# A linear-attention and mixture-of-experts kernel: where g tiles and raw weights lie, the order of the first 16 slots, and the diagonals of the first units on ScalarE

## Chip, core and metric

One core of a Trainium2 chip runs the whole program in one launch. The metric is the device time of that core in microseconds, median over runs.

## What is computed

Three stages over 3072 tokens (4 sequences of 768, 8 heads of 48):

```
for t in range(S):                                   # stage 1, per batch and head
    y[t]  = r[t] @ (state + outer(u * k[t], v[t]))
    state = w[t][:, None] * state + outer(k[t], v[t])
x = y as [3072, 384]
h = x @ w_in                                         # stage 2, 384 -> 2048 -> 384
x1 = (h * tanh(softplus(h))) @ w_out
logits = x1 @ w_gate                                 # stage 3, 8 experts, 384 tokens each
assign tokens to experts greedily, largest logit first, until an expert is full
out[mask_e] = relu(x1[mask_e] @ w1[e]) @ w2[e]
```

## The kernel before, in words

**Units.** Stage 1 is cut into 24 units of 128 columns (two sequences side by side, 64 steps each). `att0` (L341) makes running products of w by a scan on VectorE and the product `rk`; `att_inv` their inverses on ScalarE; `att1` and `att1b` scale r and k in place; `att_K` transposes k into `kn`; `att_A` multiplies k with r into PSUM tile `A`; `bon1` and `bon2` make the bonus terms `bT` and `bt`; a tile `Dt` is built as a diagonal (identity times `bt`, L387) into which `copy_predicated` puts the masked part of `A`; `att_S` moves the state on; `att4` (y, L463) multiplies `Dt` with v, writes the unit's outputs as two f16 halves into `xg` and starts the loads of later units.

**Weights.** `w_in` and `w_out` arrive as f64 in 16 slices. `conv` (L491) turns a slice into f32 with three VectorE instructions; `split` (L500) writes the f16 high half on ScalarE (L504) and the low half on VectorE (L505). Slices 0 to 7 give `wi`, 8 to 15 give `wo`. A raw slice lies in a buffer that `raw_of` (L243) chooses: 2 to 5 in the still empty `wo`, 6 to 9 in tiles of pool `p_g`, 0, 1 and 10 to 15 in a ring of two in pool `p_cv`. `og_T` (L517) and `og_M` (L529) multiply w_out with w_gate, so that eight more columns of `wo` give logits.

**Slots.** Tokens are taken in 12 groups of 256 (two units each). A slot is one eighth of a group's first layer: `mm1` (L547), 18 matmuls with 256 columns, then a tanh and a scaled copy. Four slots make a half, on which `act_ln`, `act_sin`, `act_he` and `act_g` (L568 to L601) leave the tile `g` as f16 high and low. The second layer is a stream of 384 parts (`mm2_part`, L605), three matmuls each, 32 to a group; `mm2` (L719) draws from it after each slot so many as the tables `rate` and `beat` say. For groups below `ND0` a part has 392 columns, of which eight are the logits `V`; for the others `logits` (L634) and `logits_sum` (L652) compute these apart.

**Order.** Nothing is scheduled by a tool. Every step has a key in slots, in the table `CFG`; all steps are sorted by it (L752) and written out in that order, which each engine follows. `CFG["dve"]` says for each kind of small copy which indices go to VectorE; the rest go to ScalarE. `warm` (L334) issues dummy matmuls of 512 columns on TensorE, 108 in all. TensorE's first 37 have nothing else in front.

**Gate and experts.** After the last slot, `gate` finds thresholds by 22 rounds of counting, `make_idx` writes the token index of each expert slot, both on VectorE with small matmuls; at each of their pauses TensorE takes some of the remaining parts (`amount`). The index then drives gathers of x1 rows, 30 dummy matmuls (`hold`) and the eight experts.

Of the kernel before, what the change touches and what calls it, by code (L numbers as in the profile page):

```python
# [18 lines left out]
P = 128  # L19
# [4 lines left out]
CFG = {'conv': [-27.465, -26.239, -0.642, 0.355, 1.387, 1.774, 3.754, 5.116, 5.48, 6.31, 6.977, 7.807, 8.631, 10.369,  # L24
          10.592, 11.496],
 'split': [-27.205, -24.825, 0.807, 1.381, 2.26, 3.003, 4.163, 5.354, 5.902, 7.352, 7.913, 8.296, 8.882, 11.157,
           11.265, 12.47],
 'ogT': [6.752, 8.458, 9.9, 10.25, 11.129, 11.882, 12.619, 12.917],
 'ogM': [8.177, 9.662, 10.2, 10.602, 11.386, 11.899, 12.819, 14.749],
 'u': ({'att0': -3.415,  # L30
        'bon1': -2.42,
        'bon2': -0.705,
        'inv': 1.465,
        'r1': 1.47,
        'k1': 1.491,
# [24 lines left out]
        1: {'att0': -20.044,  # L60
            'inv': -19.909,
            'r1': -19.677,
            'bon1': -19.214,
            'k1': -18.359,
            'K': -17.218,
            'A1': -17.179,
            'bon2': -18.264,
            'S': -16.813,
            'y': -15.438},
        2: {'att0': -19.14,  # L70
            'inv': -18.95,
# [36 lines left out]
            'A1': 6.016,
            'S': 7.667},
        6: {'att0': -3.862, 'bon1': -2.537, 'bon2': -0.898},  # L110
        7: {'att0': -1.258, 'bon1': -1.188, 'bon2': -0.407}},
 'rate': [(9, 0), (16, 20), (78, 200), (81, 201), (89, 209), (88, 219), (93, 232), (99, 258)],
 'beat': (16, 80, (9, 3, 0, 0, 2, 0, 0, 7)),
 'close_cv': 15.0,
 'close_att': 86.65,
 'mm1': 0.724,
 'mm2': 1.324,
 'half': ({'at': -2.795, 'sin': (-0.016, -0.015), 'he': (0.269, 0.464), 'g': (1.712, 3.088)},
          {'at': -0.109, 'sin': (0.379, 0.536), 'he': (0.613, 1.164), 'g': (3.652, 5.128)}),
 'halves': {},  # L120
 'begin': {('warm', 0): -33.78,
           ('wg',): 5.6,
           ('ld', 4): -25.706,
           ('ld', 5): -25.98,
           ('ld', 6): -24.091,
           ('ld', 7): -21.7,
           ('ld', 8): -23.6,
           ('ld', 9): -23.974,
           ('warm', 1): -24.946,
           ('warm', 2): -24.041,  # L130
           ('warm', 3): -1.989,
           ('warm', 4): 4.794,
           ('warm', 5): 9.244,
           ('warm', 6): 9.808},
 'warm': [37, 12, 14, 20, 15, 2, 8],
 'amount': {'I0': 3, 'I1': 0, 'g': 1, 't': 6, 'c': 3, 'o': 11},
# [7 lines left out]
         'ghi': {33, 4, 37, 5, 9, 13, 45, 17, 21, 25, 29, 31},  # L144
# [7 lines left out]
 'alone': {9},  # L152
 'lg': 7.167,
 'hold': 30}
# [3 lines left out]
def tile_rwkv_mish_greedy_moe(  # L158
# [47 lines left out]
    p_o = ctx.enter_context(tc.tile_pool(name="p_o", bufs=2, side="right"))  # L206
    p_cv = tc.tile_pool(name="p_cv", bufs=1, side="right")
# [35 lines left out]
    def raw_of(i):  # L243
        if 2 <= i < 6:
            t = spare[:, (i - 2) * KD * CW:(i - 1) * KD * CW]
        elif 6 <= i < 10:
            t = p_g.tile([P, 2, NF // 2, G], F16, name="g").rearrange("p a f g -> p (a f g)")
            t = t.bitcast(mybir.dt.int64)[:, 0:KD * CW]
        else:
            t = pc.tile([P, KD * CW], mybir.dt.int64, name="raw", bufs=2)  # L250
        return t
# [89 lines left out]
    def att0(n):  # L341
# [8 lines left out]
        (nc.vector if on_v("rk", n) else nc.gpsimd).tensor_tensor(rk, Tps["r", n], Tps["k", n], op=ALU.mult)  # L350
# [28 lines left out]
    def bon2(n):  # L379
        pb = pq.tile([P, C], F32, name="Y", bufs=2)  # L380
        made.add("whole")
        nc.tensor.transpose(pb, bTs.pop(n), ident)
        bt = pa.tile([P, 2, NP], F32, name="bt")
        move("bT", n, bt, pb.rearrange("t (p j) -> t j p", j=32)[:, 0:2, :])
        bt = bt.rearrange("t j p -> t (j p)")
        Dt[n] = pa.tile([P, H, L], F32, name="Dt")
        (nc.vector if on_v("Dt", n) else nc.gpsimd).tensor_tensor(Dt[n], diag[:, None, :].to_broadcast([P, H, L]),  # L387
                                bt[:, :, None].to_broadcast([P, H, L]), op=ALU.mult)

    def att1b(n):  # L390
# [3 lines left out]
        (nc.vector if on_v("nt", n) else nc.gpsimd).tensor_tensor(nt, inv, E_of(n)[:, :, 1:], op=ALU.mult)  # L394
# [67 lines left out]
    def att4(n):  # L462
# [838 lines left out]
```

## Time and profile before

| | us |
|---|---|
| median of 3 runs | 836.95 (836.71 to 838.04) |
| profiled execution, own time | 836.1 |
| its span | 834.4 |
| TensorE matmul busy | 762.4 (91%) |
| VectorE busy | 548.4 (66%) |
| ScalarE busy | 452.8 (54%) |
| mean granted TensorE clock | 0.956 of full |

The profile's shares are averages over stages. The text on the rows goes by stretches of the span: the start up to the slot where TensorE is full (0 to 151 us), the slots (to 497), the gate (to 616), the experts (to the end). A clock of 1.00 means 2.4 GHz and 0.50 means 1.2 GHz.

### The profile page before, as it was taken

The page shows a single profiled execution, that of the slowest core. Times are in us where ns is not written, and L with a number is a line of the kernel's source. Part 1 is how long each engine was busy: PE and PEld are TensorE (multiplying, and loading weights), DVE is VectorE, ACT ScalarE, POOL GpSimd, SP SyncE. Part 2 cuts the span into 40 slices and gives each one's busy share as a digit, 9 for nine tenths or more (in the row PEclk, how much of TensorE's full clock was granted, in tenths as well). Part 3 has the DMA queues.
Part 4 walks back from the last instruction along what each step waited for, and adds up shares of the span by engine and source line. Part 5 has one row for each costly group of instructions (what it writes and reads, how often), then busy time and mean ns, then how long its engine had stood idle before and what let it go on. Part 6 is the DMA issues. An engine that isn't in the chain of part 4 may idle for free. (4 is left out here: it accounts for less than half of the span.)

```text
span 834.4 us, 20144 instructions
## 1 busy us (share of the span) xinstructions
PE 762.4 (91%) x8825; PEld 523.3 (63%) x8825; DVE 548.4 (66%) x971; ACT 452.8 (54%) x658; POOL 58.7 (7%) x98
## 2 busy tenths in 40 slices
PE   7768678899999999999999998999869999999996
PEld 4455456677687777777778774555545555655563
DVE  6898985578796887977966325777745553355520
ACT  2246775858788687786877765010015554345521
POOL 0000000000000000000000010000020233122211
PEclk9798789999999999999999998999959999999998
DMA  7852331041231422313200104000424543555100
GB/s 291 237 186 45 101 90 43 15 89 43 52 78 29 88 49 45 78 45 72 49 18 10 25 11 161 20 20 21 169 62 161 196 134 136 180 193 192 60 29 28
DMA packets 22219, 74.11 MB, mean 89 GB/s; under 512 B 4496, under 2 KB 13072, under 8 KB 20080
## 3 DMA queue, kind: packets, MB, share of 16 engines
q1 hardware_dynamic: 19056, 63.35, 25.8%
q0 software_dynamic: 3072, 9.44, 3.6%
q8 instruction: 71, 1.16, 0.6%
q14 instruction: 20, 0.16, 0.1%
HBM read 62.15 MB, written 9.44 MB: 86 GB/s over the span
## 5 line engine op out<-in xcount | busy, mean ns | idle before, releaser
L561 PE MATMUL Hp<-xg,wi 128*128 128x256 f16 x1728 | 211.1, 279 | 1.4 <-DMA xg<-xg 1.4
L616 PE MATMUL X<-wo,g 128*128 128x392 f16 (+1 forms) x1152 | 210.9, 332 | 0.6 <-ACT wT L329 0.6
L561 PEld LDWEIGHTS <-wi 128*128 128x128 f16 x1728 | 168.2, 100 | 30.8 <-DMA xg<-xg 2.2
L616 PEld LDWEIGHTS <-g 128*128 128x128 f16 x1152 | 108.9, 99 | 68.2 <-issue 4.2
L565 ACT ACTIVATE es<-Hp 128x512 f32<-128x512 f32 x96 | 57.1, 594 | 97.6 <-PE Hp L561 97.0
L1146 PE MATMUL Hp<-xe,a 128*128 128x384 f16 (+1 forms) x612 | 100.9, 316 | 6.4 <-DVE hT L1151 5.2
L1163 PE MATMUL X<-a,hT 128*128 128x384 f16 x576 | 97.2, 326 | 0.0
L1146 PEld LDWEIGHTS <-a 128*128 128x128 f16 x612 | 57.7, 98 | 48.4 <-issue 14.5
L1163 PEld LDWEIGHTS <-hT 128*128 128x128 f16 x576 | 56.3, 98 | 34.8
L588 DVE TENSOR_TENSOR hs<-hs,es 128x1024 f32<-128x1024 f32 x48 | 56.0, 1219 | 33.0 <-ACT es L580 33.0
L1151 DVE SCALAR_TENSOR_TENSOR hT<-Hp,hT 128x384 f16<-128x384 f32 x64 | 35.3, 553 | 46.8 <-ACT hT L1150 46.8
L601 DVE TENSOR_TENSOR g<-hs,g 128x1024 f16<-128x1024 f32 x48 | 57.7, 1220 | 8.3 <-ACT g L329 7.9
L1092 DVE SCALAR_TENSOR_TENSOR a<-stg,a 128x1024 f16<-128x1024 f32 (+4 forms) x56 | 59.6, 1066 | 3.2 <-ACT a L1089 2.7
L1166 ACT ACTIVATE or<-X 128x384 f32<-128x384 f32 x24 | 11.8, 490 | 81.0 <-issue 60.7
L1128 DVE SCALAR_TENSOR_TENSOR xe<-cn,xe 128x384 f16<-128x384 f32 x24 | 13.3, 555 | 61.0 <-ACT xe L1127 60.9
L1089 ACT ACTIVATE a<-stg 128x1024 f16<-128x1024 f32 (+4 forms) x56 | 50.9, 926 | 1.7 <-DMA stg<-in_w_dram 1.7
L580 ACT ACTIVATE es<-es,right 128x1024 f32<-128x1024 f32 x48 | 51.5, 1138 | 0.1
L329 ACT ACTIVATE x1o<-X 128x384 f32<-128x384 f32 x12 | 5.8, 485 | 80.4 <-PE X L616 53.0
L1150 ACT ACTIVATE hT<-Hp 128x384 f16<-128x384 f32 x64 | 31.4, 490 | 32.9 <-PE Hp L1146 31.8
L275 ACT ACT_TABLE_LOAD x37 | 47.5, 1283 | 1.5 <-PEq L1285 0.8
L573 ACT ACTIVATE es<-es,mid__121 128x2048 f32<-128x2048 f32 x24 | 48.0, 2000 | 0.3
L329 ACT ACTIVATE hs<-Hp 128x512 f32<-128x512 f32 x76 | 45.0, 592 | 0.0
(189 smaller groups left out, 890.6 us busy)
## 6 DMA issues: line engine op xcount, KB each, us to landing
stg<-in_w_dram SPq DMA_DIRECT2D x16, 1536.0 KB, 7.5
T<-in_rkw_dram SPq DMA_DIRECT2D x42, 289.5 KB, 4.8
v<-in_v_dram SPq DMA_DIRECT2D x24, 192.0 KB, 2.5
raw<-in_w_out_dram SPq DMA_DIRECT2D x6, 768.0 KB, 4.5
x_dram<-x1o SPq DMA_DIRECT2D x48, 96.0 KB, 2.2
wo<-in_w_in_dram SPq DMA_DIRECT2D x4, 768.0 KB, 9.7
raw<-in_w_in_dram SPq DMA_DIRECT2D x2, 768.0 KB, 7.6
g<-in_w_in_dram SPq DMA_DIRECT2D x2, 768.0 KB, 8.1
```

Of the source, the lines that this page charges most:

```text
L329: nc.scalar.activation(dst, src, AF.Copy, scale=scale)
L561: nc.tensor.matmul(h[:, fi, :], wi[:, a, kk, f * P:(f + 1) * P], xg[g][:, b, kk, :], start=(n == 0), stop=(n == 3 * KD - 1))
L565: nc.scalar.activation(es[g, hf][:, 2 * q:2 * q + 2, :], h, AF.Tanh, scale=0.5 / (SX * SWI))
L573: nc.scalar.activation(e, e, AF.Arctan, scale=-0.5, bias=mid_)
L580: nc.scalar.activation(e, e, AF.Sin, scale=-2.0, bias=right)
L588: nc.vector.tensor_tensor(h, h, e, op=ALU.mult)
L601: (nc.vector if on_v("glo", 2 * H_ + q) else nc.gpsimd).tensor_tensor(gt[:, 1, sl], h, gt[:, 0, sl], op=ALU.subtract)
L616: nc.tensor.matmul(x, gt[:, a, ff, m * P:(m + 1) * P], wo[:, b, f, 0:n], start=(f == 0 and i == 0), stop=(f == NF - 1 and i == 2))
L1089: nc.scalar.activation(dst[:, 0], src, AF.Copy, scale=sc_)
L1092: nc.vector.scalar_tensor_tensor(dst[:, 1], src, sc_, dst[:, 0], op0=ALU.mult, op1=ALU.subtract)
L1146: nc.tensor.matmul(ps[:, cs], a1[:, a, kk, f * P:(f + 1) * P], x[:, b, kk, cs], start=(n == 0), stop=(n == 3 * KD - 1))
L1163: nc.tensor.matmul(ps, h[:, a, f, ms], a2[:, b, f, :], start=(n == 0), stop=(n == 3 * NF2 - 1))
```

## The change

- **Pools.** A third pool `p_g2a` of two g tiles is opened ahead of `p_cv`. Raw slices 0, 1 and 10 to 15 lie in its tiles. `p_g2` shrinks from four tiles to two. Groups 0 and 1 modulo 4 take g from `p_g`, 2 from `p_g2a`, 3 from `p_g2`; the last two groups from `p_g3` as before.
- **Diagonals.** For units 0 to 4 and 6 `Dt` is built on ScalarE by eight copies of 64 columns with a per-partition scale, in place of one VectorE instruction.
- **Keys.** Nearly all keys change. Dummy matmuls fall from 108 to 78 (37 to 27 in the first block, 83 to 63 ahead of slot 0). Second-layer parts no longer begin at slot 9; 18 come in one block ahead of slot 16, where 20 had come piece by piece. 227 parts, not 240, stand ahead of the last slot.
- **Logits.** `nd0` is 7 instead of 8, so group 7 gets its logits apart.
- **Gate.** `amount` takes 5 parts for 6 at the pauses "t" and up to 15 for 11 at "o".
- **Engines.** VectorE makes 26 of 48 high halves of g (12 before), 23 of 96 `hs` (20), 3 of 24 `xg` high halves (11), 8 of 24 `x1` (12), 2 of 24 `kn` (1), 1 of 24 `bT`/`bt` pairs (5).

```diff
+    p_g2a = tc.tile_pool(name="p_g2a", bufs=2, side="right")
+    pg2a = p_g2a.__enter__()
     p_cv = tc.tile_pool(name="p_cv", bufs=1, side="right")
...
-        elif 6 <= i < 10:
-            t = p_g.tile([P, 2, NF // 2, G], F16, name="g").rearrange("p a f g -> p (a f g)")
-            t = t.bitcast(mybir.dt.int64)[:, 0:KD * CW]
         else:
-            t = pc.tile([P, KD * CW], mybir.dt.int64, name="raw", bufs=2)
+            pool = p_g if 6 <= i < 10 else pg2a
+            t = pool.tile([P, 2, NF // 2, G], F16, name="g").rearrange("p a f g -> p (a f g)")
+            t = t.bitcast(mybir.dt.int64)[:, 0:KD * CW]
...
-        (nc.vector if on_v("Dt", n) else nc.gpsimd).tensor_tensor(Dt[n], diag[:, None, :].to_broadcast([P, H, L]),
-                                bt[:, :, None].to_broadcast([P, H, L]), op=ALU.mult)
+        if on_v("Dt", n):
+            nc.vector.tensor_tensor(Dt[n], diag[:, None, :].to_broadcast([P, H, L]),
+                                    bt[:, :, None].to_broadcast([P, H, L]), op=ALU.mult)
+        else:
+            for i in range(H):
+                nc.scalar.activation(Dt[n][:, i], diag, AF.Copy, scale=bt[:, i:i + 1])
...
-            pool = pg3[0] if key[0] >= NG - 2 else (p_g, pg2[0])[key[0] // 2 % 2]
+            pool = pg3[0] if key[0] >= NG - 2 else (p_g, p_g, pg2a, pg2[0])[key[0] % 4]
...
-        cms["g2"] = tc.tile_pool(name="p_g2", bufs=4, side="right", reuse_waits="tile")
+        cms["g2"] = tc.tile_pool(name="p_g2", bufs=2, side="right", reuse_waits="tile")
...
- 'rate': [(9, 0), (16, 20), (78, 200), (81, 201), (89, 209), (88, 219), (93, 232), (99, 258)],
- 'beat': (16, 80, (9, 3, 0, 0, 2, 0, 0, 7)),
+ 'rate': [(21, 0), (16, 18), (62, 192), (80, 199), (96, 228), (98, 250)],
+ 'beat': (16, 81, (9, 3, 0, 0, 1, 0, 1, 8)),
- 'warm': [37, 12, 14, 20, 15, 2, 8],
- 'amount': {'I0': 3, 'I1': 0, 'g': 1, 't': 6, 'c': 3, 'o': 11},
+ 'warm': [27, 6, 11, 19, 10, 1, 4],
+ 'amount': {'I0': 3, 'I1': 0, 'c': 3, 'g': 1, 'o': 15, 't': 5},
- 'nd0': 8,
+ 'nd0': 7,
```

How the order moves, at three places. VectorE from `rk` of unit 1 on (`cv` are the steps of `conv`, `S` the state, `T_89` and `T_92` unit 1's k), before:

```order
L350 TENSOR_TENSOR rk<-T_89 128x512
L365 TENSOR_TENSOR T_89<-T_89,E_139 128x512
L456 TENSOR_TENSOR S_140<-Y,E_136 128x4x48 x2
L387 TENSOR_TENSOR Dt<-diag,bt 128x512
L423 COPY_PREDICATED Dt<-mask,A 128x512
L496 TENSOR_SCALAR cv_292<-raw 128x768
L497 SCALAR_TENSOR_TENSOR cv_293<-raw,cv_292 128x768
L498 SCALAR_TENSOR_TENSOR cv_293<-raw,cv_293 128x768
L394 TENSOR_TENSOR E_139<-inv,E_139 128x8x64
```

and now:

```order
L355 TENSOR_TENSOR rk<-T_92 128x512
L465 TENSOR_TENSOR S_143<-Y,E_139 128x4x48 x2
L505 TENSOR_SCALAR cv_243<-g 128x768
L506 SCALAR_TENSOR_TENSOR cv_244<-g,cv_243 128x768
L507 SCALAR_TENSOR_TENSOR cv_244<-g,cv_244 128x768
L505 TENSOR_SCALAR cv_253<-g 128x768
L506 SCALAR_TENSOR_TENSOR cv_254<-g,cv_253 128x768
L507 SCALAR_TENSOR_TENSOR cv_254<-g,cv_254 128x768
L370 TENSOR_TENSOR T_92<-T_92,E_142 128x512
L432 COPY_PREDICATED Dt<-mask,A 128x512
L403 TENSOR_TENSOR E_142<-inv,E_142 128x8x64
```

The first `Dt` has left the queue, and two weight slices are converted where one was.

ScalarE over the same stretch (`inv` is `att_inv`, `wi` a slice's high half), before:

```order
L329 ACTIVATE kn<-Y 128x512
L357 ACTIVATE inv<-E_139 128x512
L358 ACTIVATE inv<-inv 128x512
L329 ACTIVATE bT<-Y 128x128
L329 ACTIVATE bt<-Y 128x8
```

and now:

```order
L334 ACTIVATE kn<-Y 128x512
L334 ACTIVATE bT<-Y 128x128
L334 ACTIVATE bt<-Y 128x8
L397 ACTIVATE Dt<-diag,bt 128x64 x8
L362 ACTIVATE inv<-E_142 128x512
L363 ACTIVATE inv<-inv 128x512
L334 ACTIVATE bT<-Y 128x128
L513 ACTIVATE wi<-cv_254 128x3x256
L513 ACTIVATE wi<-cv_244 128x3x256
L334 ACTIVATE bt<-Y 128x8
L397 ACTIVATE Dt<-diag,bt 128x64 x8
```

Eight copies for a diagonal now stand ahead of unit 1's inverses and of the weight halves.

TensorE at the end of the gate (`tri`, `ones`, `OH` are weights of the index matmuls), before:

```order
L1040 LDWEIGHTS tri
L1040 MATMUL cn<-cp,tri 128x8
L953 LDWEIGHTS ones
L953 MATMUL tp<-cp,ones 128x8
L1062 LDWEIGHTS OH
L1062 MATMUL cn<-Q,OH 128x24
```

and now, where the last two rows stand 30 times (ten parts) ahead of the matmuls with `OH`:

```order
L1052 LDWEIGHTS tri
L1052 MATMUL cn<-cp,tri 128x8
L965 LDWEIGHTS ones
L965 MATMUL tp<-cp,ones 128x8
L625 LDWEIGHTS g
L625 MATMUL X<-wo,g 128x384
```

Ten second-layer parts now follow the count of the assigned tokens; before, all were done ahead of it.

## Rows read from the trace of the kernel before

**Rows 1.** By stretch: busy us of PE, PEld, DVE, ACT, POOL, then TensorE clock, DMA share, GB/s
```profile
75.00:100.00 25.00, 15.51 (x204) 11.48 (x202) 23.68 (x38) 18.75 (x26) 0.00 (x0) 0.78 0.21 69
...
125.00:150.00 25.00, 21.78 (x349) 16.82 (x350) 12.46 (x21) 12.89 (x25) 0.00 (x0) 1.00 0.21 46
...
150.00:500.00 350.00, 339.65 (x4859) 258.70 (x4858) 253.59 (x377) 265.40 (x353) 2.38 (x16) 1.00 0.21 47
...
525.00:600.00 75.00, 74.36 (x864) 43.64 (x861) 55.73 (x202) 5.77 (x13) 0.00 (x0) 1.00 0.16 47
...
600.00:620.00 20.00, 10.95 (x74) 7.51 (x72) 11.84 (x49) 0.49 (x1) 3.98 (x4) 0.62 0.31 96
```

**Rows 2.** Timeline of TensorE: start, length, line, what; its idle time before
```profile
2.09 10.69 PE L339 MATMUL Y<-first,id 128*128 128x512 f16 x37 [2.09 <-POOL first L296]
...
44.89 2.14 PE L561 MATMUL Hp<-xg,wi 128*128 128x256 f16 x18
...
81.52 4.05 PE L561 MATMUL Hp<-xg,wi 128*128 128x256 f16 x18
...
133.08 0.50 PE L524 MATMUL X<-id,wo 128*128 128x128 f16 x6 [1.17 <-ACT wT L329]
...
150.80 2.13 PE L561 MATMUL Hp<-xg,wi 128*128 128x256 f16 x18
```

**Rows 3.** Timeline of VectorE, the two long waits before the first slot
```profile
13.65 0.69 DVE L350 TENSOR_TENSOR rk<-T 128x512 f32<-128x512 f32 x1 [2.65 <-PE Y L375]
...
33.36 0.69 DVE L327 TENSOR_SCALAR xg<-A 128x512 f16<-128x512 f32 x1 [2.91 <-PE A L473]
```

**Rows 4.** Timeline of VectorE, the last split of a weight slice
```profile
128.39 0.95 DVE L505 SCALAR_TENSOR_TENSOR wo<-cv,wo 128x768 f16<-128x768 f32 x1
```

**Rows 5.** Groups by line, whole run: count, then busy us, mean ns, idle before and its releasers
```profile
L387 DVE TENSOR_TENSOR Dt<-diag,bt 128x512 f32<-128x512 f32 x24 | 16.5, 688 | 7.6 <-ACT bt L329 7.3
...
L601 DVE TENSOR_TENSOR g<-hs,g 128x1024 f16<-128x1024 f32 x48 | 57.7, 1220 | 8.3 <-ACT g L329 7.9
...
L327 DVE TENSOR_SCALAR wT<-X 128x768 f16<-128x768 f16 x4 | 2.2, 552 | 0.9 <-PE X L524 0.9
...
L347 DVE TENSOR_TENSOR_SCAN E<-T,first 128x520 f32<-128x520 f32 x24 | 29.6, 1234 | 0.3
...
L350 DVE TENSOR_TENSOR rk<-T 128x512 f32<-128x512 f32 x24 | 16.0, 668 | 3.2 <-PE Y L375 2.6 <-DMA T<-in_rkw_dram 0.6
...
L329 ACT ACTIVATE bT<-Y 128x128 f32<-128x128 f32 x19 | 5.1, 270 | 4.7 <-PE Y L375 4.0 <-PE Y L382 0.8
...
L329 ACT ACTIVATE bt<-Y 128x8 f32<-128x8 f32 x19 | 3.3, 174 | 4.7 <-PE Y L382 4.6
...
L643 PE MATMUL Hp<-g,wo 128*8 128x256 f16 x192 | 7.1, 288 | 3.4 <-DVE g L327 1.9 <-DVE g L601 1.6
```

**Rows 6.** Timeline of TensorE, end of the slots
```profile
458.61 1.48 PE L643 MATMUL Hp<-g,wo 128*8 128x256 f16 x48
...
462.50 0.51 PE L655 MATMUL Hp<-pick,lgt 128*128 128x8 f32 x4
...
494.76 2.13 PE L561 MATMUL Hp<-xg,wi 128*128 128x256 f16 x18
...
497.09 9.10 PE L616 MATMUL X<-wo,g 128*128 128x392 f16 x54
```

**Rows 7.** Timeline of VectorE, start of the gate
```profile
518.64 0.28 DVE L872 TENSOR_REDUCE sc<-tp 1x1 f32<-1x128 f32 x1 [2.44 <-PE tp L871]
...
521.57 0.56 DVE L327 TENSOR_SCALAR x1o<-X 128x384 f32<-128x384 f32 x1 [2.65 <-PE X L616]
```

**Rows 8.** Timeline of all engines, end of the gate
```profile
603.04 0.17 PE L1040 MATMUL cn<-cp,tri 128*128 128x8 f16 x1 [0.73 <-DVE cp L945]
...
606.53 1.32 PE L1062 MATMUL cn<-Q,OH 128*128 128x24 f16 x6 [3.30 <-DVE OH L1057]
...
613.51 1.13 POOL L1113 DMA_INDIRECT xr<-x_dram,idx  x1 [113.89 <-DVE idx L1064]
```

More of the change, by code (lines that the diff above doesn't have):

```diff
@@ new lines @@
+CFG = {'conv': [-28.559, -28.796, -9.197, -0.926, 0.696, 1.907, 2.814, 4.759, 2.932, 5.667, 6.934, 7.118, 8.281, 10.201,
+          10.159, 10.891],
+ 'split': [-27.728, -26.98, -0.788, 1.233, 2.549, 2.564, 3.442, 5.926, 5.381, 6.383, 8.239, 9.176, 8.901, 10.848,
+           10.815, 11.802],
+ 'ogT': [6.61, 8.484, 9.185, 9.828, 11.404, 11.777, 11.841, 12.734],
+ 'ogM': [8.421, 8.977, 10.284, 11.259, 11.757, 11.949, 12.856, 14.904],
+ 'u': ({'att0': -3.966,
+        'bon1': -2.332,
+        'bon2': -0.558,
+        'inv': 0.952,
+        'r1': 1.588,
+        'k1': 1.685,
+        'K': 2.45,
+        'A1': 2.696,
+        'S': 3.749,
+        'y': 3.949},
+       {'att0': -1.229,
+        'bon1': -0.513,
+        'bon2': -0.149,
+        'inv': 1.626,
+        'r1': 1.639,
+        'k1': 1.921,
+        'K': 4.751,
+        'A1': 5.483,
+        'S': 6.515,
+        'y': 6.939}),
+ 'un': {0: {'att0': -22.788,
+            'inv': -17.308,
+            'r1': -16.39,
+            'bon1': -16.099,
+            'k1': -16.3,
+            'K': -16.194,
+            'A1': -15.42,
+            'bon2': -15.914,
+            'S': -15.982,
+            'y': -12.998},
+        1: {'att0': -20.243,
+            'inv': -19.686,
+            'r1': -19.528,
+            'bon1': -18.89,
+            'k1': -18.743,
+            'K': -16.924,
+            'A1': -16.644,
+            'bon2': -17.142,
+            'S': -16.887,
+            'y': -15.917},
+        2: {'att0': -20.678,
+            'inv': -20.431,
+            'r1': -19.952,
+            'bon1': -18.723,
+            'k1': -18.761,
+            'bon2': 3.038,
+            'K': 3.349,
+            'A1': 6.221,
+            'S': 4.573,
+            'y': 7.494},
+        3: {'att0': -22.38,
+            'inv': -22.177,
+            'r1': -18.58,
+            'bon1': 0.141,
+            'k1': -17.652,
+            'bon2': 2.777,
+            'K': 4.196,
+            'A1': 4.231,
+            'S': 4.546,
+            'y': 6.865},
+        4: {'K': 5.098,
+            'A1': 4.967,
+            'S': 6.755,
+            'y': 6.767,
+            'att0': -0.274,
+            'bon1': 1.78,
+            'bon2': 3.836,
+            'inv': 2.253,
+            'r1': 3.598,
+            'k1': 3.921},
+        5: {'y': 8.271,
+            'att0': -1.728,
+            'bon1': 2.608,
+            'bon2': 3.299,
+            'inv': 3.137,
+            'r1': 3.756,
+            'k1': 4.797,
+            'K': 5.788,
+            'A1': 6.305,
+            'S': 6.995},
+        6: {'att0': -3.549, 'bon1': -2.42, 'bon2': -0.165},
+        7: {'att0': -1.811, 'bon1': -0.009, 'bon2': 0.497}},
+ 'rate': [(21, 0), (16, 18), (62, 192), (80, 199), (96, 228), (98, 250)],
+ 'beat': (16, 81, (9, 3, 0, 0, 1, 0, 1, 8)),
+ 'close_cv': 13.929,
@@ L115 @@
  'close_att': 86.65,
  'mm1': 0.724,
[L117 to L134, printed above, removed]
@@ L135 @@
- 'warm': [37, 12, 14, 20, 15, 2, 8],
- 'amount': {'I0': 3, 'I1': 0, 'g': 1, 't': 6, 'c': 3, 'o': 11},
[7 rows of a table added]
+ 'begin': {('warm', 0): -39.26,
+           ('wg',): 6.961,
+           ('ld', 4): -26.892,
+           ('ld', 5): -25.134,
+           ('ld', 6): -25.457,
+           ('ld', 7): -23.796,
+           ('ld', 8): -22.44,
+           ('ld', 9): -20.592,
+           ('warm', 1): -25.415,
+           ('warm', 2): -23.65,
+           ('warm', 3): -2.595,
+           ('warm', 4): 6.275,
+           ('warm', 5): 3.182,
+           ('warm', 6): 5.161},
@@ L619, in put_logits @@
     def put_logits(g, m, x):
+        made.add(("V", g * MG + m))
         nc.vector.tensor_scalar(V[:, g * MG + m, :], x, 1.0 / (SG * SWO), None, op0=ALU.mult)
@@ L655, in logits_sum @@
             nc.tensor.matmul(l[:, m], t[:, m * P:(m + 1) * P], pick, start=True, stop=True)
+        made.update(("V", g * MG + m) for m in range(MG))
         nc.vector.tensor_scalar(V[:, g * MG:(g + 1) * MG, :], l, 1.0 / (SG * SWO), None, op0=ALU.mult)
@@ L770, in tile_rwkv_mish_greedy_moe @@
     logits_sum(NG - 1)
+    need(*(("V", t) for t in range(NTT)))
     p_moe.__exit__(None, None, None)
@@ L1197, in tile_rwkv_mish_greedy_moe @@
     p_g2.__exit__(None, None, None)
+    p_g2a.__exit__(None, None, None)
     p3 = ctx.enter_context(tc.tile_pool(name="p3", bufs=2, side="right", reuse_waits="tile"))
```

109 lines of the change are left out of this document (13 added, 96 removed), and 18 rows, old and new, of the table CFG.

## The prediction, made before the change was run

> **What bounds the kernel now.** I read the busy times by stretch first. From 150 to 500 us TensorE is busy 339.65 of 350 us at full clock, in the counting of the gate 74.36 of 75 [rows 1]: there only less TensorE work, or TensorE work moved out, gains time. Before 150 it is different: from 75 to 100 VectorE is busy 23.68 of 25 us and TensorE 15.51, at a mean clock of 0.78; from 125 to 150 VectorE has fallen to 12.46 [rows 1]. So the start is a chain through VectorE that ends when the last weight slice is split, at 129.3 [rows 4]. The third place is 600 to 620, where TensorE is busy 10.95 of 20 us [rows 1], because it waits for the index.
>
> Then TensorE's timeline. I use two marks in the start. M is the end of the last `og_T` transposes, 133.6; S is the start of slot 16's first-layer matmuls, 150.80 [rows 2]. At both marks both kernels have, by their orders, done the same first-layer slots (0 to 12, 0 to 15) and the same steps of the units; only second-layer parts and dummies differ. Behind M TensorE is nearly full, so S follows from M by adding up work.
>
> **The start, up to M.** VectorE's queue up to the last split is shorter. By the two orders, five `Dt` (units 0 to 4) have left it, 5 x 0.688; two low halves of g (2 x 1.22), one scan (1.23) and one `rk` (0.67) now stand behind the split; two `wT` fewer are VectorE's (2 x 0.55) [rows 5]. That is 8.9 us, and a little less since neighbours in the queue overlap: **8.0 us**. What moved behind the split costs nothing there, since VectorE is idle half of 125 to 150 [rows 1].
>
> Next the waits. VectorE waited 2.65 us for TensorE to finish the first dummies and free `rk`, and 2.91 us for y of unit 1, ahead of which stand 12 dummies [rows 3]. The first 37 took 10.69 us [rows 2], 0.29 each, so ten fewer end 2.9 earlier and the first wait goes. Six dummies instead of 12, and three VectorE instructions put in between, leave about 0.5 of the second. **5.0 us** gained; none at worst, if the chain through ScalarE takes the place.
>
> New waits are the unknown cost. A diagonal on ScalarE is eight copies of 64 columns; no row shows one. The nearest are 0.174 us at 8 columns and 0.270 at 128 [rows 5], so eight take 1.4 to 2.2, five diagonals 7 to 11 us, in a queue that also makes the weight halves and the inverses VectorE needs. ScalarE is busy 18.75 of 25 us in its fullest window of the start [rows 1], so most of it falls into idle time, and in the order shown two conversions on VectorE cover the first diagonal. The bounds are 0 and 11; nearer to the low end, by that idle share, I take **3.0 us**. The early loads shift too (two w_out slices now stand ahead of unit 3's inputs), but that unit is needed after unit 2's chain, and I take this in with the 3.0.
>
> So M = 133.6 - 8.0 - 5.0 + 3.0 = 123.6.
>
> **From M to S.** Before, 17.2 us, in which 12 parts were done (8 stood ahead of M). Now all 18 stand there: six more. A part is 9.10/18 = 0.5 us [rows 6], so 3.0 more, and S = 123.6 + 17.2 + 3.0 = 143.8. That is **-7.0**. The block of 18 needs the whole g of half 0 and 1, whose last low half is about 9 us of VectorE work behind the last split; TensorE reaches the block some 11 us behind M, so it is there.
>
> **Dummies.** Thirty fewer save only the wait above: 20 of them stand ahead of slot 0, the rest where TensorE idles anyway. Their other use is the clock. The rows show that a slot's 18 matmuls take 2.14 us at full clock and 4.05 at half [rows 2], and that half-clock stretches occur with all 108 present. The Trainium skill (TensorE: Matmul & The Clock Gate, section "What's actually happening") says that the throttled state is the default and activity releases it, which speaks against this change. By that rule the start would give back what it gains and the sum would end above the time before; by the rows, denser slots replace the dummies as activity, and I charge nothing. The rule is the third rival.
>
> **Slot 16 to the last slot.** By the orders, 220 parts before, 209 now: 11 x 0.5 = 5.5 less. Group 7's logits apart cost TensorE 1.48 + about 0.2 to start them, and less than 0.51 for the sum [rows 6]: about 2.0. Eight columns fewer in 32 parts give back 0.2. Together **-3.7**. The copies that changed engine cost nothing: in the slots VectorE is busy 253.59 and ScalarE 265.40 of 350 [rows 1], and the balance moves by under 15 us. If that cover were gone, TensorE would wait for an evacuation in every slot.
>
> **Behind the last slot.** Its matmuls start at 494.76 [rows 6], and from there a chain over tanh, sine, the products and g ends about 17 us later; TensorE fills this with 18 parts and still waits 3.4 us for g, summed over the logits groups [rows 5]. Now 24 parts fill it: six more, 3.0 us, in the hole. **0**; the bound is 3.0 if the hole is less. At the gate's start VectorE waits 2.44 and 2.65 us for TensorE [rows 7], which works off six parts each time; five each give **-1.0**.
>
> **End of the gate.** Ten parts, 5.0 us, now follow the count matmul at 603.04. TensorE sits idle 3.30 there and then follows VectorE's `OH` at VectorE's pace until the first gather at 613.51 [rows 8]. They end about 608.3 and the 24 index matmuls catch up. **0**; the bound is +5 if they run at half clock. The last x1 rows are written about 2 us ahead of the gather.
>
> **Pools.** Nothing: group 2 needs `p_g2a` at about slot 25, long after raw slice 15 is converted, and each later group takes a tile whose reader is eight slots gone.
>
> **Sum.** -7.0 - 3.7 - 1.0 = -11.7, on the profiled execution's 836.1: 824.4. The median of the runs stands 0.85 above that execution, so 825.2; I say **825.0**.
>
> **Rivals.**
>
> *The start does not get shorter.* The diagonals' copies delay weight halves at the upper bound (11 for 3), or loads do the like: M 131.6, S 151.8, a loss of 1.0 against the 4.7 gained behind S: 836.1 - 3.7 + 0.85, about 833.3. For it: every engine serves short chains in order there. Against it: ScalarE's idle share. 0.15.
>
> *The ten late parts hold up the gather.* The clock is at 0.62 in 600 to 620 [rows 1]. At half clock ten parts take 10 us and the index comes 5 later: 830. Against it: the low clock there follows idle time that they fill. 0.08.
>
> *TensorE at half clock in the start, slower than before.* Thirteen slots stand ahead of M; each at half clock costs 4.05 - 2.14 = 1.9 more, 25 in all, beyond those that are slow already. The gains behind S are 4.7, so this decides from S = 155.5, M = 135.3, that is from 12 us of slowing that nothing covers; with 16 uncovered, S is 159.8 and the time 841. For it: 0.78 with all dummies. Against it: the slots come closer together. The Trainium skill's page on the clock gate, cited above, would make this the likelier case. 0.07.
>
> *The change does not do what it says, in one place:* the hole behind the last slot is not there to fill and the gains cancel to within 0.2%, with half the start lost too: 0.02 by itself.
>
> **Numbers.** My forecast, a start shorter by 4 to 13 us, has 0.68. The range: with no new waits 822; with every gain at its bound and the idle before the experts shorter by the faster clock 817.5. Upwards the first two rivals reach 833.5. So 817.5 to 833.5; outside it lie the third rival and tails. Faster by over 0.2% (1.7 us, about what a measurement of this kernel can tell from no change): 0.68 and the first two rivals, less tails, 0.87; within 0.2% 0.06; slower 0.07.
>
> **What would show it.** Right: S near 144; VectorE without the two waits of rows 3; the last split near 119; logits of the last group with almost no wait of TensorE; the first gather about 11 to 12 us earlier, at the same distance from the count matmul as before. Wrong: new waits of VectorE for ScalarE's weight halves or of `copy_predicated` for `Dt`; clock at 0.5 in slots 0 to 12; the distance from the count matmul to the gather longer than before.

## The result and the profile after

Median of four runs **801.15 us** (800.11 to 801.94) against 836.83 of the kernel before: ratio 0.957, 95% interval 0.955 to 0.959. The forecast was 825.0, between 817.5 and 833.5. The direction was right, the size three times too small. The two profiled executions differ by 834.4 - 800.2 = 34.2 us of span:

| stretch | before | after | change | forecast |
|---|---|---|---|---|
| start to S (slot 16) | 150.80 | 132.77 | -18.0 | -7.0 |
| S to the last slot's first layer | 343.96 | 327.77 | -16.2 | -3.7 |
| from there to the count matmul | 108.28 | 105.82 | -2.5 | -1.0 |
| count matmul to first gather | 10.47 | 10.36 | -0.1 | 0 |
| first gather to expert 0's second layer | 23.1 | 25.7 | +2.6 | 0 |
| from there to the end | 197.8 | 197.8 | 0 | 0 |

Timelines of the changed kernel at the places of [rows 2, 4], columns as there (L533 is `og_T`, L514 the last split, L570 the first layer, L625 a second-layer part):

```profile
110.09 0.95 DVE L514 SCALAR_TENSOR_TENSOR wo<-cv,wo 128x768 f16<-128x768 f32 x1
...
112.28 0.83 PE L533 MATMUL X<-id,wo 128*128 128x128 f16 x12
...
123.70 9.13 PE L625 MATMUL X<-wo,g 128*128 128x392 f16 x54
132.66 0.27 PE L387 MATMUL Y<-ident,bT 128*128 128x128 f32 x1
132.77 2.13 PE L570 MATMUL Hp<-xg,wi 128*128 128x256 f16 x18
```

The last split ends at 111.0 (129.3 before), M is 113.1 (133.6; forecast 123.6), and from M to S it takes 19.7 us (forecast 20.2). All of the start's surprise therefore lies ahead of M. VectorE, from the start to the end of the last split, first of the kernel before and then of the changed one (columns as in [rows 1]):

```profile
0.00:129.30 129.30, 96.76 (x1305) 64.64 (x1306) 110.99 (x172) 66.80 (x105) 1.72 (x10) 0.84 0.49 153
```
```profile
0.00:111.00 111.00, 82.04 (x1259) 58.94 (x1260) 102.43 (x161) 76.27 (x146) 1.72 (x10) 0.87 0.57 179
```

It is busy 8.6 us less, as the order said (8.0), and idle 18.3 - 8.6 = 9.7 us less, where the forecast had 2.0 (5.0 gained, 3.0 lost). Its two long waits of [rows 3] are 0.47 and 1.20 now, and the waits for ScalarE's weight halves (1.8 for `wi` and 1.8 for `wo` before, each two times 0.9) are gone:

```profile
10.87 0.69 DVE L355 TENSOR_TENSOR rk<-T 128x512 f32<-128x512 f32 x1 [0.47 <-PE Y L380]
...
30.22 0.69 DVE L332 TENSOR_SCALAR xg<-A 128x512 f16<-128x512 f32 x1 [1.20 <-PE A L482]
```

In the slots TensorE was idle 10.35 us before and is 1.1 now. Its waits from slot 16 to the last slot (us in total, times, longest), before and after:

```profile
PE Y L433 <- DVE T L398: 5.9, 6, 3.0
PE Y L375 <- DVE rk L350: 2.8, 7, 0.9
PE Hp L561 <- DMA xg<-xg: 1.4, 2, 0.8
```
```profile
PE Hp L570 <- DMA xg<-xg: 0.3, 1, 0.3
PE Hp L665 <- ACT lgt L334: 0.3, 1, 0.3
```

The K transposes waited for the unit's last product `T`, the bonus matmuls for `rk`. The windows that answer to [rows 1] show the same: 347.28 of 350 us busy in the slots; 600 to 620 now lies in the experts.

```profile
75.00:100.00 25.00, 16.59 (x306) 13.51 (x305) 23.73 (x38) 23.18 (x39) 0.00 (x0) 0.86 0.43 129
...
150.00:500.00 350.00, 347.28 (x4931) 259.97 (x4929) 262.63 (x408) 250.24 (x347) 2.38 (x16) 1.00 0.23 55
525.00:600.00 75.00, 66.33 (x648) 42.09 (x647) 49.66 (x164) 14.10 (x24) 5.95 (x7) 0.91 0.26 82
600.00:620.00 20.00, 19.52 (x123) 12.04 (x122) 6.70 (x12) 7.11 (x14) 5.75 (x7) 1.00 0.44 163
```

At the gate's end the ten late parts stand where TensorE waited 3.30 [rows 8], and the index matmuls (L1074) catch up:

```profile
566.36 0.17 PE L1052 MATMUL cn<-cp,tri 128*128 128x8 f16 x1 [1.22 <-DVE cp L957]
...
566.41 5.04 PE L625 MATMUL X<-wo,g 128*128 128x384 f16 x30
571.28 4.13 PE L1074 MATMUL cn<-Q,OH 128*128 128x24 f16 x24
579.83 2.61 PE L1222 MATMUL cn<-OH,ones 128*128 128x128 f16 x23 [4.41 <-PEq L1215]
583.12 0.93 PE L1222 MATMUL cn<-OH,ones 128*128 128x128 f16 x7 [0.69 <-issue]
```

The last two rows are the 30 holding matmuls behind the branch. Their gap of 0.69 is new and comes up again below. Line numbers of an experiment's kernel are its own; the names tell what is meant.

### The profile page after: what moved, and what is told of

Same layout as the page of the kernel before. It is cut to its first block, busy times and chain, and to the rows that moved or that the text cites. A ratio compares the mean times of both kernels' runs of the same rounds, so it can differ in the third digit from the quotient of the medians.

```text
span 800.2 us, 20251 instructions
## 1 busy us (share of the span) xinstructions
PE 748.7 (94%) x8848; PEld 519.3 (65%) x8848; DVE 546.7 (68%) x962; ACT 457.3 (57%) x711; POOL 58.7 (7%) x98
## 5 line engine op out<-in xcount | busy, mean ns | idle before, releaser
L570 PE MATMUL Hp<-xg,wi 128*128 128x256 f16 x1728 | 208.4, 277 | 0.4 <-DMA xg<-xg 0.3
L625 PE MATMUL X<-wo,g 128*128 128x392 f16 (+1 forms) x1152 | 208.4, 328 | 0.0
L570 PEld LDWEIGHTS <-wi 128*128 128x128 f16 x1728 | 167.2, 99 | 28.5 <-issue 0.9
L625 PEld LDWEIGHTS <-g 128*128 128x128 f16 x1152 | 107.1, 98 | 65.7 <-issue 0.9
L334 ACT ACTIVATE x1o<-X 128x384 f32<-128x384 f32 x16 | 7.8, 490 | 81.9 <-PE X L625 52.0
L334 ACT ACTIVATE hs<-Hp 128x512 f32<-128x512 f32 x73 | 43.3, 592 | 0.0
```

The source lines that it names most:

```text
L334: nc.scalar.activation(dst, src, AF.Copy, scale=scale)
L570: nc.tensor.matmul(h[:, fi, :], wi[:, a, kk, f * P:(f + 1) * P], xg[g][:, b, kk, :], start=(n == 0), stop=(n == 3 * KD - 1))
L625: nc.tensor.matmul(x, gt[:, a, ff, m * P:(m + 1) * P], wo[:, b, f, 0:n], start=(f == 0 and i == 0), stop=(f == NF - 1 and i == 2))
```

## The start: which part of the change shortened it

**The diagonals back on VectorE** (changed kernel).

```diff
-         'Dt': {5, 7, 8, ..., 23},
+         'Dt': {0, 1, 2, ..., 23},
```

> The changed kernel with all diagonals back on VectorE. Theory A (the start is VectorE's queue, counted instruction by instruction): five diagonals stand ahead of the last split again, 5 x 0.69 = 3.4 us, so the last split ends at 114.4 instead of 111.0, slot 16 starts at 136.2 instead of 132.8, and the time is 801.2 + 3.4 = 804.6. Rival B (the copies on ScalarE hold up other work there): undoing them gives back what it costs, the time stays within 1 us of 801.2. Rival C (relieving VectorE is what took its short waits away): the waits for ScalarE's weight halves come back, slot 16 at 139 or later, time 807 or more.

801.83 us (ratio to before 0.959, 95% interval 0.957 to 0.961; so in all that follows), S 132.8, last split 111.6. Up to the last split VectorE is busy 2.8 us more, of which 2.2 come out of its idle time (8.6 to 6.4):

```profile
0.00:111.60 111.60, 83.45 (x1264) 59.46 (x1265) 105.22 (x166) 67.15 (x106) 1.73 (x10) 0.85 0.56 178
```

Theory A falls: of the queue's 8.0 us, the diagonals' 3.4 are worth 0.6 at the last split and nothing at S. B's number came out, and its reason in part: VectorE waits for no copy of ScalarE's in the changed kernel, but TensorE's waits up to S for ScalarE's `kn`, `bT` and `wT`, there 3.6, 2.2 and 5.3, are 1.3, 0.4 and 2.5 with the diagonals back, while its wait for `Dt` grows from 3.6 to 8.0. What the diagonals took from one queue they put on another.

**The new order of the first 16 slots alone** (kernel before), and **the old order back** (changed kernel): `conv`, `split`, `ogT`, `ogM`, `begin`, `halves`, `warm` and the units' exceptions `un`; in the first also the early entries of `rate`, so that 20 parts stand ahead of slot 16.

```diff
-CFG = {'conv': [-27.465, -26.239, -0.642, ...
+CFG = {'conv': [-28.559, -28.796, -9.197, ...
...
- 'rate': [(9, 0), (16, 20), ...
+ 'rate': [(21, 0), (16, 20), ...
```

> The kernel before with the new order of the first 16 slots and the new dummies alone; pools, diagonals on VectorE and the choice of engines are the old ones. Theory A (the order took VectorE's waits away, without help from the rest): slot 16 starts at 132.8 + 3.4 for the diagonals + about 1 for two weight transposes' copies = 137, 13.6 us earlier than before, and with nothing changed behind it the time is 836.8 - 13.6 = 823. Rival C (the order needs the diagonals on ScalarE or the pools): slot 16 at 145 or later, time 831 or more.

> The changed kernel with the old order of the first 16 slots and the old dummies; diagonals on ScalarE, pools and choice of engines are the new ones. Theory A: the diagonals alone take 3.4 us and the copies' move about 1 off VectorE's queue, slot 16 at 146.4 instead of 132.8, time 801.2 + 13.6 = 815. Rival C (the diagonals, not the order, took the waits): slot 16 at 142 or earlier, time 810 or less.

The order alone: 819.69 (0.980, 0.978 to 0.983), S 138.6, M 116.1. Theory A holds at S, but for 1.6 us; another 4.1 were gained in the slots. The old order back: 821.29 (0.982, 0.979 to 0.984), S 154.0. So the order (with its dummies) is worth 12.2 of the 18.0 at S and 17.5 of the 20.5 at M by itself, and 21.2 at S when it is taken out; without it the rest gains nothing at S. Its last split is at 113.7, and up to there, with the diagonals on VectorE, VectorE's idle time is 7.3 us where it was 18.3, and its two long waits are short:

```profile
0.00:113.70 113.70, 84.23 (x1260) 59.40 (x1261) 106.36 (x168) 65.62 (x103) 1.72 (x10) 0.84 0.57 174
```
```profile
DVE xg L404 <- PE A L550: 1.4, 1, 1.4
DVE rk L427 <- PE Y L452: 0.5, 1, 0.5
```

Which of the keys that make up the order does this was not taken apart. In the old order, with the diagonals on ScalarE, VectorE's waits up to its last split (at 127.5) include the ones that the prediction feared:

```profile
DVE rk L426 <- PE Y L451: 3.2, 1, 3.2
DVE wi L585 <- ACT wi L584: 2.9, 3, 1.1
DVE xg L403 <- PE A L553: 2.8, 1, 2.8
DVE Dt L503 <- ACT Dt L468: 2.4, 1, 2.4
DVE wo L585 <- ACT wo L584: 2.3, 3, 1.0
```

**The new numbers of dummies alone** (kernel before), and **no later dummies** and **15 first ones and no others** (changed kernel).

```diff
- 'warm': [37, 12, 14, 20, 15, 2, 8],
+ 'warm': [27, 6, 11, 19, 10, 1, 4],
```
```diff
- 'warm': [27, 6, 11, 19, 10, 1, 4],
+ 'warm': [27, 0, 0, 0, 0, 0, 0],
```
```diff
- 'warm': [27, 6, 11, 19, 10, 1, 4],
+ 'warm': [15, 0, 0, 0, 0, 0, 0],
```

> The kernel before with the new numbers of dummies alone (27, 6, 11, 19, 10, 1, 4 for 37, 12, 14, 20, 15, 2, 8). The prediction's term of 5.0 us for the two waits: VectorE's wait of 2.65 for the first dummies goes, of its 2.91 for y of unit 1 some 1.2 are left (six dummies x 0.29 fewer), slot 16 at 146.5, time 832.5. Rival S (the chain of the start absorbs it elsewhere): slot 16 within 1 us of 150.8, time 836. Rival D (clock): first slots at half clock, time 838 or more.

> The changed kernel without the 51 dummies of groups 1 to 6; the first 27 stay. Theory A (the slots themselves hold the clock, the dummies fill idle time): the granted clock in the windows from 25 to 125 us stays within 0.03 of 0.90, 0.93, 0.86, 0.86, and the time is within 1.5 us of 801.2. Rival D (the clock hangs on the dummies): first-layer slots take 4.05 instead of 2.14 us in part of the start; with five slots or more at half clock that nothing covers, slot 16 comes 5 to 25 us later and the time is 806 or more.

> The changed kernel with 15 of its first 27 dummies and none of the 51 later ones (those 51 gone gave 797.2). Theory A (dummies only stand ahead of work in TensorE's queue): VectorE's wait of 0.47 us for the first dummies goes too, time 796 to 797.5. Rival D (the first dummies bring the clock up): half clock for longer in the first 25 us, slot 16 later than 130.2 by 1 us or more, time 798 or more.

The new numbers alone: 833.76 (0.996, 0.994 to 0.998), S 147.46; VectorE's wait for the first dummies is 1.25 instead of 2.65, the one for y 2.15 instead of 2.91. So the term of 5.0 was worth 3.3, and rivals S and D fall. None of the later ones: **797.17** (0.953, 0.951 to 0.955), S 130.2, 2.5 earlier; 15 alone: 797.03 (0.952, 0.950 to 0.955), S 130.8. Two kernels below that leave the changed kernel's start as it is have S at 131.4 and 131.9 instead of 132.8, so about 1 us of the 2.5 is within the spread of executions. The time gained is more than S accounts for, because the stretch behind the gather is 23.1 us here and 25.7 in the changed kernel (see below). Theory A falls with the clock, and rival D with the time: the clock falls, but nothing gets slower. Without the dummies the window from 25 to 50 us and slot 0 read:

```profile
25.00:50.00 25.00, 15.80 (x299) 12.28 (x292) 23.70 (x36) 13.22 (x34) 0.00 (x0) 0.65 0.85 245
```
```profile
39.18 3.83 PE L644 MATMUL Hp<-xg,wi 128*128 128x256 f16 x18
```

Granted clock 0.65 where the changed kernel has 0.90, and slot 0 at the lower level (3.83 instead of 2.14), yet S is earlier: in this window TensorE waits for others, 3.3 us for VectorE's `Dt` and 3.7 for ScalarE's `kn`, `bt` and `bT`. The third rival's price, time lost with each slot at half clock, was not paid. By the Trainium skill (TensorE: Matmul & The Clock Gate, section "What's actually happening") the throttled state is the default and activity releases it. The trace agrees with that: fewer dummies, a lower clock.

## The slots: where TensorE's idle time went

**The inverse's key alone** and **the choice of engines alone** (kernel before).

```diff
-        'inv': 1.465,
+        'inv': 0.952,
```
```diff
-         'x1': {2, 3, 4, 5, 6, 7, 8, 10, 14, 16, 20, 22},
+         'x1': {2, 3, 4, 5, 6, 7, 8, 16},
...
-         'x0': {1, 5, 8, 9, 11, 13, 15, 17, 19, 21, 23},
+         'x0': {8, 1, 15},
```

> The kernel before with one number changed: the inverse of an even unit of the steady slots is issued at 0.952 instead of 1.465, as in the changed kernel. Theory G (TensorE's idle time in the slots is the K transposes' wait for VectorE's last product, which waits for ScalarE's inverse): from slot 16 to the last slot TensorE's 10.35 us of idle time fall to about 4.5, the waits of the K transposes (5.9) vanish, and the time is 836.8 - 6 = 831. Rival H (they wait because VectorE has too much in its queue): nothing changes, 836 to 837.

> The kernel before with the changed kernel's choice of engines for the evacuations and copies (x0 and x1 to ScalarE, more high halves of g to VectorE); diagonals and all keys are the old ones. Rival H (VectorE's queue is too long in the slots): the idle time of TensorE from slot 16 to the last slot falls from 10.35 us to 4 or less, time 830. Theory G (it is the order of issue): idle time 9 to 12 us, and no change in the slots; the start may gain up to 1.1 us by two weight transposes' copies: 835.5 to 837.

The inverse's key: 836.79 (1.000, 0.997 to 1.002), the waits for `T` and `rk` at 6.7 and 3.1, so theory G falls and H's number comes out. The choice of engines: 846.61 (1.008, 1.006 to 1.011), slower, with S 4.9 later and 13.7 us of idle time behind it, so H falls, and G's numbers with it.

**One of three parts put back** (changed kernel): the steady units' keys `u`; the keys `half` and `mm2`; the choice of engines.

```diff
- 'u': ({'att0': -3.966, 'bon1': -2.332, ...
+ 'u': ({'att0': -3.415, 'bon1': -2.42, ...
```
```diff
- 'half': ({'at': -2.101, 'sin': (0.091, 0.228), ...
+ 'half': ({'at': -2.795, 'sin': (-0.016, -0.015), ...
```
```diff
-         'x0': {8, 1, 15},
+         'x0': {1, 5, 8, 9, 11, 13, 15, 17, 19, 21, 23},
```

> The changed kernel with the old keys of the units' ten steps in the steady slots (units 6 to 23); all else new. Theory N (the units' keys place bon1 and the K transposes behind their VectorE inputs): TensorE's waits for rk (about 2.8 us) and for T (about 5.9) come back between slot 16 and the last slot, that stretch is 336 instead of 327.8, time 809. Rival P (the tanh and g steps' keys or the choice of engines took them away): 327 to 330, time 801 to 803.

> The changed kernel with the old keys of the steps of a half (es, sines, products, g) and of the second-layer parts; the exceptions for halves 0 to 3 stay. Rival P (these keys took the waits away, since they stand on ScalarE and VectorE ahead of the inverse): slot 16 to last slot 333 us or more with waits of TensorE for T, time 806 or more. Theory N: 327 to 329, time 801 to 802.5.

> The changed kernel with the old choice of engines for evacuations and copies (x0, x1 and bT back to VectorE in part, fewer high halves of g there); the diagonals stay on ScalarE. The same choice alone made the kernel before 9 us slower. Theory Q (the choice fits only the keys that it came with): undoing it costs here as well, 5 us or more, with TensorE's waits in the slots back. Rival R (it is a burden in either order): time 801 or less. Between: 802 to 804, it hardly matters once the keys are right.

The units' keys: 810.8 (0.967, 0.963 to 0.972), idle 10.4. The half's: 815.51 (0.973, 0.969 to 0.978), idle 9.4. The choice of engines: 815.36 (0.974, 0.970 to 0.979), idle 5.2. The main waits of the first two, from slot 16 to the last slot:

```profile
PE Y L454 <- DVE rk L429: 9.1, 8, 1.9
```
```profile
PE Hp L739 <- ACT lgt L408: 5.1, 3, 3.8
PE Y L454 <- DVE rk L429: 2.1, 5, 0.5
```

Each costs 10 to 14 us, so none of the parts is the cause by itself, and what N and P expected of each other's run (no cost) falls. Their waits are not the ones expected either: with the old units' keys only the wait for `rk` is back (the one for `T` is 0.2), with the old half's keys TensorE waits most for the copy of the logits, `lgt`, and not for `T`. Q's number holds, but of its cost 4.7 us lie ahead of S (137.5), 7.0 in the slots. The shares of the three are thus not shares of the same 9.2 us.

**The three together, with the beat** (kernel before), and **the old pacing back** (changed kernel): `beat`, `rate`, `nd0`, `lg`, `lg2` and `amount`.

```diff
- 'beat': (16, 80, (9, 3, 0, 0, 2, 0, 0, 7)),
+ 'beat': (16, 81, (9, 3, 0, 0, 1, 0, 1, 8)),
```
```diff
- 'beat': (16, 81, (9, 3, 0, 0, 1, 0, 1, 8)),
+ 'beat': (16, 80, (9, 3, 0, 0, 2, 0, 0, 7)),
```

> The kernel before with all that the change does to the steady slots and nothing of the start: keys of units 6 to 23, keys of a half and of the second-layer parts, the beat, and the choice of engines (diagonals stay on VectorE). Undone one at a time in the changed kernel each of the three costs 10 to 14 us; the inverse's key alone gave 0 and the choice of engines alone lost 9. Theory V (they work only together): TensorE's idle time from slot 16 to the last slot falls from 10 us to 3 or less, that stretch gets 7 us shorter or more, time 830 or less, some us of which the choice of engines may give back in the start. Rival W (they need the new start as well): idle time 7 or more, time 834 or more.

> The changed kernel with the old pacing of the second-layer parts and the gate: 20 parts ahead of slot 16, old beat and rate, logits apart from group 8 on, 6 and 11 parts per stage of the gate. By the prediction's terms the slots get 3.7 longer and the gate 1.0: 806. Theory Z (the pacing is part of what keeps TensorE's inputs ready; it is what the slots' edits alone lacked in the kernel before): TensorE's idle time from slot 16 to the last slot 4 us or more where it is 1.1, time 808 or more. Rival (pacing moves work and no waits): idle time below 2.5, time 804 to 807.

The three alone: 839.99 (1.0035, 1.001 to 1.006), idle 8.1: rival W by its number. The waits for `rk` and the short ones for `T` that came back every eight slots are gone. What is left is nearly all the K transposes' wait, four times; the one without a releaser starts 0.1 us behind the end of `T` as well, at the place where the kernel before waited 3.0:

```profile
PE Y L507 <- DVE T L472: 5.0, 3, 1.7
PE Y L507 <- issue: 2.6, 1, 2.6
```

The old pacing back: 815.22 (0.975, 0.972 to 0.978), idle 8.4, theory Z. TensorE's waits in it, slot 16 to the last slot, are those of the kernel before:

```profile
PE Y L516 <- DVE T L481: 5.2, 7, 2.2
PE Y L454 <- DVE rk L429: 2.6, 7, 0.5
PE Hp L644 <- DMA xg<-xg: 0.6, 2, 0.4
```

In eight slots the new beat holds 22 parts, the old 21. That the extra half microsecond of TensorE work lies just where it waited 0.34 for `rk` and 0.5 for `T` is argued, not shown. With the old start and everything else new (the run with the old order back), TensorE's idle time in the slots is 2.1, so they don't need the new start; which smallest set they need stays open.

**The old pools back** (changed kernel).

```diff
-        else:
-            pool = p_g if 6 <= i < 10 else pg2a
+        elif 6 <= i < 10:
+            t = p_g.tile([P, 2, NF // 2, G], F16, name="g").rearrange("p a f g -> p (a f g)")
...
+        else:
+            t = pc.tile([P, KD * CW], mybir.dt.int64, name="raw", bufs=2)
```

> The changed kernel with the old pools: the ring of raw weight slices back in the conversion pool, g tiles by turns of two groups from two pools of four. The prediction charged nothing for the pools. Theory T (nothing): 801 to 803. Rival U (the new pools let the late slices load earlier, or free g tiles sooner): waits of VectorE for raw slices in the start or of g's steps in the slots, 804 or more.

801.25 (0.958, 0.955 to 0.961), S 132.6, idle 1.2: theory T, the pools carry nothing.

## Behind the gather: the 2.6 us given back

**Dummies ahead of the branch**, **the ten late parts ahead of the count matmul**, **30 tiny matmuls at the very start** (changed kernel).

```diff
     more(1000)
+    bridge = pgs.tile([P, P], F32, name="cn")
+    for _ in range(60):
+        nc.tensor.matmul(bridge[:, 0:P], ones, OH[:, 0], start=True, stop=True)
```
```diff
     for kind in make_idx(check):
-        more(amount[kind])
+        more(1000)
```
```diff
             nc.tensor.matmul(wps, id16, warm_rhs, start=True, stop=True)
+        for _ in range(30 if n == 27 else 0):
+            nc.tensor.matmul(wps[:, 0:8], id16, warm_rhs[:, 0:8], start=True, stop=True)
```

> The changed kernel with 60 dummies of 128 columns behind the index matmuls, ahead of the branch at which TensorE then sits idle for 4.4 us. Theory K (the experts' first 25 us are 2.6 us longer than before because the granted clock falls to 0.50 in that idle time and comes back at 589.5 only, 13 us behind the gather instead of 8): the clock stays near 1.00, the distance from the first gather to the first matmul of the second layer of expert 0 falls from 25.7 to 23.1 or less, time 798.5 or less. Rival L (the rows of x1 that are written late, or the gather's landing, set that stretch): 25 to 26 us as now, time 801. Rival M (the dummies delay what is behind them): more than 26.5, time 802 or more.

> The changed kernel with the ten second-layer parts that follow the count matmul put ahead of it. Theory K: TensorE sits idle behind the count matmul as in the kernel before, its clock falls there and is back earlier behind the gather, so that the first gather's distance to the first matmul of expert 0's second layer is 23.1 again instead of 25.7; the count matmul itself comes later by what of the 5 us its wait of 1.2 doesn't cover, 3.8: time 801.2 + 3.8 - 2.6 = 802.4. Rival L (late writes of x1): the writes come earlier too, so the stretch falls as well, but the clock in 576 to 590 is as now.

> The changed kernel with 30 matmuls of 8 columns more behind its first 27 dummies, where TensorE has nothing else to do. In every kernel whose 30 holding matmuls behind the branch show a gap of 0.6 to 1.5 us (released by nothing that the profile shows, after the 23rd in five kernels with the same number of TensorE instructions ahead, after the 20th in one), the clock comes back late and the gather stands 25 us or more ahead of expert 0's second layer; in those without a gap it is 22.4 to 23.3. Theory X (the gap belongs to the place in TensorE's instruction stream): 30 instructions more move it out of the holding matmuls, the distance is 23.1 or less, time 801.2 - 2.5 = 798.7. Rival Y (the ten late parts or the late x1 rows make it): gap and distance as now, 25.7, time 801 to 802.

The bridge (the 60 dummies): 802.63 (0.956, 0.953 to 0.958) and 29.0 us from the gather to the second layer, rival M. The clock fell in the index matmuls already, so the 60 ran 6.15 us, and the branch's 3.8 us began only behind them:

```profile
574.30 6.15 PE L1284 MATMUL cn<-OH,ones 128*128 128x128 f16 x60
584.24 3.36 PE L1299 MATMUL cn<-OH,ones 128*128 128x128 f16 x30 [3.78 <-PEq L1292]
```

The late parts moved ahead: 804.46 (0.959, 0.957 to 0.961), the count matmul 3.2 later, the stretch 25.9 as before: theory K falls, and so does L. Put side by side, the runs with a gap in the 30 holding matmuls stood out, and the last of the three tested that: 30 tiny matmuls more, **799.09** (0.955, 0.953 to 0.958), no gap, 23.1 us. Theory X by its numbers. The time by itself would not show it: the interval overlaps the changed kernel's, and one of the five executions took 801.15; of the 2.8 us by which the two profiled spans differ, 2.6 lie in this stretch. The changed kernel and this one, from the gather on (columns as above; the clock is the third number from the end):

```profile
582.70:584.70 2.00, 1.58 (x12) 1.58 (x12) 0.00 (x0) 0.00 (x0) 0.00 (x0) 0.50 0.20 74
584.70:586.70 2.00, 1.67 (x13) 1.30 (x13) 1.11 (x2) 0.98 (x2) 1.43 (x2) 0.50 0.10 16
586.70:588.70 2.00, 2.00 (x19) 1.94 (x18) 0.00 (x0) 0.19 (x1) 0.54 (x2) 0.50 0.60 174
588.70:590.70 2.00, 2.00 (x30) 2.00 (x29) 0.56 (x1) 0.30 (x1) 0.00 (x0) 0.75 0.02 6
```
```profile
580.50:582.50 2.00, 2.00 (x22) 2.00 (x20) 0.00 (x0) 0.00 (x0) 0.90 (x1) 0.50 0.62 150
582.50:584.50 2.00, 1.77 (x10) 1.41 (x9) 0.51 (x1) 0.89 (x2) 0.80 (x1) 0.59 0.16 61
584.50:586.50 2.00, 1.90 (x32) 1.89 (x32) 0.60 (x2) 0.52 (x2) 1.18 (x3) 1.00 0.35 98
```

With the gap the clock is back at about 589.7, 13 us behind the gather at 576.7; without it at about 584.1, 7.6 behind 576.5.

**18 holding matmuls instead of 30**, and none of the later dummies.

```diff
- 'hold': 30,
+ 'hold': 18,
```

> The changed kernel without the 51 later dummies (that alone: 797.2) and with 18 of the 30 holding matmuls behind the branch. These 30 take 3.4 us at half clock and end 6.0 us behind the first gather, whose rows land 3 to 4 us behind its issue. Theory: the first transposes start 1.2 us earlier and the clock comes back at the same moment, since TensorE stays busy: 796 to 797. Rival: with fewer matmuls the clock comes back later, and the expert's first layer takes 1 us or more longer: 797.5 or more.

**796.73** (0.952, 0.950 to 0.954). The transposes start 5.0 instead of 6.1 us behind the gather, but the clock is back later (8.4 us behind it, 7.3 with 30), and the stretch is 22.7 instead of 23.1. The theory's time comes out, but not its reason, a clock that is back at the same moment; and 796.73 is not to be told from the 797.17 with 30. These three kernels near 797 beat both kernels of this study.

## Why the prediction was right in direction and wrong in size

*The start (-7.0, measured -18.0).* The step that failed is "The start, up to M", in its second term, "5.0 us gained" for the waits. It priced two of VectorE's waits, 5.6 us, of the 18.3 us that VectorE was idle up to the last split. The new order alone takes 11.0 us of that idle time away. The two named waits gave 3.9 (3.3 at S by dummies alone); the waits for ScalarE's weight halves and others that the prediction did not list went with them. The first term was well sized: 8.6 us less busy for 8.0, and 4.6 of it in the order alone, where the steps moved behind the split were counted at 4.3. The diagonals were right in sum: counted at 3.4 gained and 3.0 lost, they took 2.8 us off VectorE's busy time and left it 2.2 more idle. As a reason for a shorter start they carry nothing. In the old order they do harm, as feared: VectorE waits 2.4 for the first one. The prediction also said that the copies that changed engine cost nothing. They are no cost here but a gain: put back, S is 4.7 later.

*M to S.* Right: 19.7 for 20.2.

*Dummies.* "I charge nothing" was wrong on the other side from the rival: the 51 that stayed cost up to 2.5 us at S.

*Slot 16 to the last slot (-3.7, measured -16.2).* This step failed too: it counted work alone and put TensorE's idle time at no change, without a reason. The busy time fell by 7.0 (the logits matmuls of one group, charged here with about 1.5 of the 2.0, stand behind the last slot), the idle time by 9.2. "Nearly full" at 339.65 of 350 [rows 1] hid 10 us that a question for TensorE's waits would have shown, and the new keys, the choice of engines and the pacing all bear on them.

*Behind the last slot, the gate, its end, the pools.* Right in kind: TensorE's wait for g falls from 3.4 to 0.3, the gather stands at the same distance, the pools carry nothing. The gate gained 2.5 for 1.0.

*The experts.* Not in the sum: 2.6 lost, with a gap in the holding matmuls whose place depends on how many TensorE instructions stand ahead, and a clock that comes back later.

## What to carry to other kernels

Where an engine is nearly full, ask for the list of its waits before pricing its work: idle time that is spread over many short waits is gained or lost by the order alone. A queue counted shorter is a gain only if the engine that serves it has no idle time behind the edit; put the piece back by itself to find out. Edits that were chosen together are undone one at a time, but their single prices don't add up (here 20 for the order, 10, 14, 14 and 14 for the slots' parts, of a whole of 36).

## What the runs showed of the hardware

A place in TensorE's instruction stream can cost time. In the changed kernel and five others with as many TensorE instructions ahead, the 30 holding matmuls stop behind the 23rd for 0.6 to 1.5 us, released by nothing that the profile shows; in the run with the old choice of engines they stop behind the 20th, for 1.5. With 51 or 63 matmuls fewer, 30 or 60 more, the old numbers of dummies or the old pacing there is no gap. The profile lists a DMA queue that carries instructions, with 71 packets in the whole run:

```profile
q8 instruction: 71, 1.16, 0.6%
```

The packets' times in the traces fit a wait for one of them. In all seven runs with the gap TensorE goes on 1.2 to 1.6 us behind the end of a packet on this queue (in the changed kernel the packet ends at 581.84, and the 24th matmul starts at 583.12). No run held back a packet by itself.

Where the gap came, the clock was back 10.9 to 13.0 us behind the gather and the stretch was 25.1 to 25.9 us long; without it 5.5 to 8.4, and 22.4 to 23.3 (the bridge apart). One execution goes against this: with the old pools the gap was 0.64, but the clock was back after 6.4 and the stretch 23.2. So the gap makes the late clock likely, not certain.

TensorE sits idle for 3.8 to 4.5 us behind its last instruction ahead of the branch, in all 20 traces, and its first matmul behind the branch starts 1.5 to 1.6 us behind the end of a packet on the same queue in each of them. Work put ahead of the branch doesn't cover this: with the 60 dummies, 6.15 us of work, the holding matmuls start 5.4 us later behind the gather (8.5 instead of 3.1).
